# Six groups of an attention kernel hand a block of exponentials from VectorE to ScalarE, in a newly written order

## The chip, the cores and the metric

The kernel runs on one core of a Trainium2 chip. Its engines are TensorE (PE, matmul), VectorE (DVE), ScalarE (ACT), GpSimd (POOL) and SyncE (SP), which here issues the DMAs. The metric is the device time of one execution in microseconds (us), the median of three runs.

## The reference

A layer norm of x (2048 tokens, 640 features) feeds two branches: attention with 32 heads of 20 features, and a gated mixer with an MLP. The output is x plus their product.

```python
xn = _layernorm(x, axis=-1)
s = _A_ref(xn, A_wqkv, A_wo)                 # 32 heads, Dh 20: softmax(q k / sqrt(20)) v, then @ wo
g = _silu(_B_ref(xn, B_w1, B_w2, B_w3, B_w4))
return x + s * g

# _B_ref(x, w1, w2, w3, w4)
h = _gelu(_layernorm(x, axis=-1) @ w1)
...
hs = jnp.concatenate([g0, g1, g2, g3], axis=-1) @ w2   # quarters of h, shifted by 1, -1, 2, -2 tokens
x1 = x + hs
h2 = _gelu(_layernorm(x1, axis=-1) @ w3) @ w4          # w3: 640 x 1536, w4: 1536 x 640
return x1 + h2
```

## The kernel before, in words

**Groups.** The 32 heads go in eight quads of four. For each quad the 2048 queries go in four chunks of 512. One (quad, query chunk) is a group; there are 32. In a group, the scores of 16 key tiles of 128 keys are formed for four heads, exponentiated and multiplied with the values into one PSUM bank, number 7, which is not shared. The other seven PSUM banks hold scores and all other products in turn. `attn_quad` (L1366) writes a group out.

**Two ways to exponentiate.** A plain key tile (`score_act`) has two exponentials on ScalarE, each over two heads by 512 queries (`exp_act`, the activation at L1684, 128x1024), and one value product of four matmuls (L1424, or L1606 for blocks). A *block* is a pair of key tiles (`BLK`) in which each tile has two heads on ScalarE and two on VectorE (`score_both`, L1690). VectorE turns scores into the bits of an approximate exponential (L1707, 128x1024, from PSUM). `block_bits` (L1571) then makes three copies of these bits with other offsets (v = 1, 2, 3) and multiplies all four versions with the values, v = 0 and 1 with weight one, the others with scaled values (`VP`): four value products for VectorE's half (L1606), one for ScalarE's half (L1424). A copy runs on GpSimd (L1592) for the versions that `PP` names, else on VectorE (L1594).

**How many blocks.** `ND[quad][qc]` is the number of blocks of a group, and `UNITS` says how they are joined: blocks one and two share one buffer (copies of 4096), so do three and four; a fifth stands alone (copies of 2048). `PP` names copies of the first and the third block only, so the fifth block's three copies are all VectorE's. `order` (L592) lays the blocks and the remaining plain tiles of a group in sequence: with five blocks six plain tiles are left, with four there are eight. Entries of `NR` from 100 up name the plain tile (by its place among them, 100 + place) whose four heads share one activation of 128x2048 (L1661) instead of two of 128x1024.

**Repeats.** `AGAIN` maps (quad, query chunk, key tile, head) to how many more times the score matmul of that head is written over the same bank (`score_pair`, L1617, `times`).

**The second branch.** `run_b` adds its stages while the attention runs: w1 beside quad 0, w2 beside quad 1, w3 and w4 from quads 2 and 4 on. Their matmuls all go through `mm_tile` (L725). For w3, a slab of 640x128 is loaded for each of 12 column tiles and four token chunks, 48 loads of 160 KB through a ring of three buffers on SP's queue (L2078, in `b_w3`). Between these loads SP also issues the copies of queries (`qm`, four issues a group, L1382), the transposes and stores of finished heads (L1750 and L1763, four stores a group) and the loads of keys and queries of the next quad.

**Order.** The whole program is a list of tasks with reads and writes. Its order on every engine, and the PSUM bank and buffer of every task, are written out in the string `TABLE` (L2133), which `follow` (L219) reads: two characters for a task, one for each resource that it takes. While reading, `follow` gives each task a planned start and end, from the costs in the task calls (`c_act`, `c_dve`, `c_pe`, numbers), from `SYNC_LAT` (planned time from an engine's end to a waiting engine), from the spacing of row-tiled matmuls (`row_at + 4.0`), and for a DMA from its bytes, a fixed latency and `dlat`. `plan_sync` (L323) draws the semaphore waits from the order and drops those that another wait implies; it sorts by planned ends. `emit` writes the instructions. So a cost constant reaches the chip only by the order that was written with it, and by which of several waits is left out.

Of the kernel before, what the change touches and what calls it, by code (L numbers as in the profile page):

```python
# [14 lines left out]
SYNC_LAT = {"pe": 225.0, "act": 158.0, "dve": 136.0, "pool": 160.0, "sp": 60.0}  # L15
# [42 lines left out]
class Planner:  # L58
# [160 lines left out]
    def follow(self, table):  # L219
# [18 lines left out]
        at = 0  # L238
# [7 lines left out]
        while at < len(table):  # L246
# [11 lines left out]
            if e == "pe" and pe_mode and t.mode:  # L258
                st = max(row_at + 4.0, *(row_end[x] for x in range(4) if t.part >> x & 1))
# [218 lines left out]
class Cfg:  # L478
# [5 lines left out]
    def __init__(self, S=2048, D=640, H=32, F=1536):  # L484
# [100 lines left out]
        self.AGAIN = {(2, 2, 6, 1): 1, (6, 0, 8, 2): 1, (6, 0, 8, 3): 1, (7, 0, 0, 0): 1, (7, 0, 0, 1): 1, (7, 0, 1, 3): 1, (7, 0, 9, 0): 2, (7, 0, 9, 1): 2, (7, 1, 1, 0): 2, (7, 1, 2, 1): 1, (7, 1, 3, 0): 3, (7, 1, 3, 1): 1, (7, 1, 5, 1): 1, (7, 1, 8, 2): 2, (7, 1, 9, 0): 1, (7, 1, 12, 2): 1, (7, 1, 12, 3): 1, (7, 1, 14, 1): 1}  # L585
# [3 lines left out]
        self.PP |= {(0, 0, 1, 3), (0, 0, 1, 2)}  # L589

# [43 lines left out]
def c_act(n):  # L634
    return 68 + 0.8333 * n
# [13 lines left out]
class Gen:  # L649
# [995 lines left out]
    def score_rows(self, b, qc, kt, wide):  # L1645
# [14 lines left out]
        T("act", c_act(2048),  # L1660
# [18 lines left out]
    def exp_act(self, hs, sa, tag):  # L1679
# [3 lines left out]
        self.T("act", c_act(1024),  # L1683
# [369 lines left out]
    def b_w3(self, c0):  # L2053
# [8 lines left out]
        for ch in (c0, c0 + 1):  # L2062
# [12 lines left out]
            for fc in range(FC):  # L2075
# [3 lines left out]
                  writes=[A("W3s", ws)], is_dma=True, nbytes=KC * 128 * 128 * 2, name=f"ld_w3_{ch}_{fc}", stream=f"w3{ws}")  # L2079
# [54 lines left out]
    r"#9#6#:#;#,#%###&#<&R#=#>#?#@#A#B#C#D#l#'#($4#-#$#E#F#Z#[#]#)#G#H#I#J#.$`#2#^#*#w#+$?&S$S#f$J#e#g#h#p%n#m$K#i$M#q#n#j#r#K#L#M#N$L$N#o#k$O#s#x#O$v#%$&#P$T#Q#R$"  # L2134
    r"P#{#|#y#_$U#b$V#`#t#a#d$Q#}#z#v#u$R#~$#$W$(#S$q$%%$6$r$s${)$t$u%&#T$|$}$w%'$l%$x$y#U$~$m%($)$X$Y$$$*$Z$n$o%#$p#V#W#X&Q$+$[#Y#c#/$]$,$'$z&[#&]&^&_&`%`'%a%b%c%"
    r"g$%d$%%h$A$-$5$&$a$.$/%p%i$_$8&a$^%)(%.%%8)%j%*%9%:%/%0%+%,%=&%e#5$7$b$9&T'%k%-$0$2$3$@%;%1%2%>%?&U%3#%@%A%4%l$:%<$B&V%f&W&X&c(&d%5%6%7$c&j%%q%m&e&f&g&k&l&m%"
    r"r&$1&n&w)&x&y%t#%u$D$C&Y$;$E%s$<&o$F$>%v%w&z&{*@$*;(*?#&h%C$G$d*<)*A%%x&|'((')'*'+$f',&6)&7*8#*9$*=)&8&9*4(*:#*5)*6(%B&:%E$e$=$g$h'-$I%D&}(&~$H$i*+$**#'#'$'%"
    r"%F$*,$%G%P%%y$j$k&;%U)%V%W'&%Q*>&<%z%H%R%K(%L%M%N%I%O%Z&%S%X%[%]%Y%{'%^%|%T%}*2(%_%J*B&*C%*1'%~&#(H(I&&$&'&(&$&)&*';&#0(G'<'='>'?&+&-&.*3'*D)*.%&%*-&&H#%o*/#"
    r"'@&,(J&2%&I&J&K&L&3*]&*^%&M*J$*_&*K#*H(*I)*E&?#&@*M&A&N&B&C*L%&D&4)'/&*P$#4+#(&5*Q%+$)+%)*S*7*0*O&*N''0'1'2*F'3'4*V)*U(&q(&r&='*R'*W(*Y&*X'&>&s&t&u+.#*f)*g(+"
    r"/$&v*T*Z$+0#*a%&i*`&*i'I#'J'K'L'M*|#*b%'N'.*j)'d*}$'e*[*~'*k(*m&*l%'5#'6'7'8'9+1$*o+2#+&*n$*c'B(':+3(*d)+?&&/+@'*e('C'D*h'*G'E'F(K'U&+4*r'V'W&E'X'G+A)+8$+9%+"  # L2140
    r":&+*(++)+P+,%'Y'O#'P'Q'R'Z*p*{'S+6%'T+5&+S#+T$+('+'(+7#']$'^+V'_'`'a+F%+G&+Z$+Y#'H'b+)$+;+C'+D(&F$*q&Z*t+H(+i%+]'A*x+E&+R#&G+h&+Q$*z+U'&O$''+~(*u+k&P,#'+-*s,"
    r"&#,%$,$#+n%+o&+q(P+I'f$,'%+X(+W'+t'g+[$'c,~'h+=#(L,@&+<$+>&,A%'['i'j*w,B('k*y'l#*v+B+_(+`)+c#+a)+J+b$'m,2&,3%,5+^'n'o+d&+l)+m('p,(,0#&p+z,1$'q+p$,8&,9%+e+f',"
    r"4%+g('r$'s#7't,>$,;,=#,6&,7%+w+K&0'u'v+j)2d+}+L'w'x#'y,?',D(,:$,M#,N$,E)'z'{'|,l%,k&,F),<,P,H#,m#,G$,I$,T(,S),C+u'},d',e&,g%'~,V,f'+x+s+r,h$,i(-1(-0)+v+M-2%,"
# [129 lines left out]
```

## Time and profile before

| | |
|---|---|
| three runs | 791.79, 790.84, 791.46 us |
| median | 791.46 us |
| the profiled execution | 791.46 us, its span (first to last instruction) 789.7 us |
| granted TensorE clock, mean | 0.998 |
| exponentials of 128x1024 on ScalarE | 718, the first at 21.9 us, the last starting at 781.7 us |
| exponentials of 128x2048 | 13 |
| conversions on VectorE (L1707) | 276 |

Busy time is that of an engine's own instructions; matmuls are pipelined and their ends are modelled, so a busy TensorE is not TensorE at its peak. ScalarE's instructions overlap a little, so its busy time counts each moment once, while the mean duration of one is longer than its spacing. "Idle before" is the time in which an engine stood before instructions of a group, with the work that ended it. The chain of waits is followed back from the last instruction. In a table by stretches each row has the stretch, its length and the busy time and instruction count of each engine in it.

### The profile page before, as it was taken

What the parts mean: (1) busy time and instruction counts of PE and PEld (TensorE: products, weight loads), DVE (VectorE), ACT (ScalarE), POOL (GpSimd) and SP (SyncE); (2) the same over time, 40 slices, a digit from 0 to 9 for tenths busy, and PEclk for the clock granted to TensorE, in tenths of its full rate; (3) what the DMA queues carried; (4) which work ended last, traced back from release to release, by engine and by line L of the source; (5) the groups of instructions that cost most, each with busy time, mean ns of one, the idle gap of its engine ahead of it and who ended that gap; (6) DMA issues with size and microseconds to landing.
All of it is one profiled execution on the core that took longest, in us unless ns stands there. A gap on an engine that the chain in (4) does not pass through costs nothing.

```text
span 789.7 us, 27655 instructions
## 1 busy us (share of the span) xinstructions
PE 774.1 (98%) x12434; PEld 292.9 (37%) x12434; DVE 702.0 (89%) x936; ACT 761.0 (96%) x791; POOL 440.3 (56%) x238
## 2 busy tenths in 40 slices
PE   8999999999999999999999999999999999998997
PEld 4433333234444333333433433233334333332454
DVE  8889888989999999988988888898989899897986
ACT  7999999999999999999999999999999999999896
POOL 5666646552655647575473645647544545536742
PEclk9999999999999999999999999999999999999999
DMA  6213633244111324333332132343340213115343
GB/s 175 47 56 103 154 82 80 63 97 106 39 27 37 55 53 89 80 62 85 62 93 54 24 71 55 70 77 62 86 101 21 49 22 92 22 19 139 86 141 109
DMA packets 141349, 58.09 MB, mean 74 GB/s; under 512 B 113728, under 2 KB 136432, under 8 KB 141232
## 3 DMA queue, kind: packets, MB, share of 16 engines
q1 hardware_dynamic: 141232, 56.33, 31.4%
q8 instruction: 97, 1.59, 0.9%
q14 instruction: 20, 0.16, 0.1%
HBM read 34.70 MB, written 10.33 MB: 57 GB/s over the span
## 4 chain that ended last, share of the span: by engine, by line
PE 76%; ACT 19%; DVE 2%; DMA 1%; SPq 1%; issue 0%
PE psum L725 28%; PE psum L1615 22%; ACT arena L1684 18%; PE psum L1606 14%; PE psum L1424 9%; PE psum L1632 1%; DVE arena L1707 1%; DMA arena<-in_A_wqkv_dram 1%; ACT arena L1661 1%; PE psum L1481 1%; SPq L912 1%; DMA arena<-in_B_w_dram 1%; PE psum L1455 0%; DVE arena L1594 0%; DVE arena L1863 0%
## 5 line engine op out<-in xcount | busy, mean ns | idle before, releaser
L1684 ACT ACTIVATE arena<-psum 128x1024 bf16<-128x1024 f32 x718 | 671.9, 1035 | 16.3 <-PE psum L1615 13.1
L1592 POOL TENSOR_TENSOR arena<-arena 128x2048 int32<-128x2048 int32 x92 | 330.0, 3598 | 187.2 <-DVE arena L1594 123.1
L1707 DVE TENSOR_SCALAR arena<-psum 128x1024 uint16<-128x1024 f32 x276 | 335.8, 1221 | 52.3 <-PE psum L1615 48.4
L725 PE MATMUL psum<-arena 128*32 128x320 bf16 (+1 forms) x5808 | 335.0, 333 | 1.5 <-DMA arena<-in_B_w_dram 0.9
L1615 PE MATMUL psum<-arena 32*128 32x512 bf16 x1956 | 261.9, 384 | 4.9 <-DVE arena L1707 2.0
L1606 PE MATMUL psum<-arena 128*22 128x512 bf16 x2208 | 191.5, 381 | 0.0
L725 PEld LDWEIGHTS psum<-arena 128*32 128x32 bf16 x5808 | 135.2, 96 | 123.8 <-issue 55.7
L1615 PEld LDWEIGHTS psum<-arena 32*128 32x128 bf16 x1956 | 69.8, 91 | 229.6 <-ACT arena L1684 127.9
L1594 DVE TENSOR_SCALAR arena<-arena 128x4096 uint16<-128x4096 uint16 (+1 forms) x139 | 140.7, 1034 | 2.1 <-PE psum L1606 1.2
L1424 PE MATMUL psum<-arena 128*22 128x512 bf16 x1432 | 136.4, 382 | 0.4 <-ACT arena L1661 0.3
L1606 PEld LDWEIGHTS psum<-arena 128*22 128x22 bf16 x2208 | 50.2, 90 | 65.0 <-issue 42.0
L1741 POOL TENSOR_TENSOR arena<-arena 128x512 bf16<-128x512 f32 x30 | 41.0, 1366 | 59.8 <-DVE arena L1594 40.7
L1424 PEld LDWEIGHTS psum<-arena 128*22 128x22 bf16 x1432 | 34.4, 90 | 47.9 <-issue 28.6
L2083 DVE CAST arena<-psum 128x512 bf16<-128x512 f32 x48 | 32.7, 683 | 3.0 <-PE psum L725 2.1
L1291 DVE CAST arena<-psum 128x512 bf16<-128x512 f32 x40 | 27.0, 682 | 2.1 <-PE psum L725 1.7
L1906 POOL TENSOR_TENSOR arena<-arena 128x640 bf16<-128x640 bf16 x12 | 16.7, 1400 | 21.4 <-DVE arena L1531 7.9
L936 DVE BATCH_NORM_STATS2 arena<-arena 128x6 f32<-128x320 bf16 x54 | 24.8, 478 | 1.0 <-DMA arena<-in_A_x_dram 1.0
L1661 ACT ACTIVATE arena<-psum 128x2048 bf16<-128x2048 f32 x13 | 24.7, 1898 | 0.8 <-PE psum L1615 0.6
L1728 DVE STREAM_TRANSPOSE arena<-psum 128x512 f32<-128x512 f32 x30 | 21.3, 710 | 2.4 <-PE psum L1606 1.2
L1840 DVE SCALAR_TENSOR_TENSOR arena<-psum,arena 128x320 bf16<-128x320 f32 x32 | 15.3, 487 | 7.8 <-PE psum L725 7.5
L953 POOL TENSOR_SCALAR arena<-arena 128x640 bf16<-128x640 bf16 x16 | 14.0, 876 | 14.5 <-DVE arena L1594 13.2
L2090 ACT ACTIVATE arena<-arena 128x6144 bf16<-128x6144 bf16 x4 | 21.1, 5316 | 0.0
(135 smaller groups left out, 330.4 us busy)
## 6 DMA issues: line engine op xcount, KB each, us to landing
arena<-in_B_w_dram SPq DMA_DIRECT2D x48, 160.0 KB, 2.8
arena<-arena SPq DMA_DIRECT2D x124, 32.0 KB, 1.9
arena<-in_B_w_dram SPq DMA_DIRECT2D x4, 960.0 KB, 5.5
arena<-in_A_x_dram SPq DMA_DIRECT2D x8, 320.0 KB, 5.6
arena<-in_A_x_dram SPq DMA_DIRECT2D x16, 160.0 KB, 2.5
out_dram<-arena SPq DMA_DIRECT2D x16, 160.0 KB, 1.9
heads<-arena SPq DMA_DIRECT2D x120, 20.0 KB, 2.0
arena<-queries SPq DMA_DIRECT2D x28, 80.0 KB
```

The lines of the kernel that those rows point to most:

```text
L725: ins = e.matmul(pb[32 * c:32 * c + 32, 0:N], lhsT(k, c), rhs(k, c), start=(k == 0), stop=(stop and k == nk - 1), tile_position=(0, 32 * c))
L1291: T("dve", c_dve(512), lambda e, h=h, c=c: e.tensor_copy(KS[:, 512 * c:512 * c + 512], self.wbank(h)[:, 0:512]), reads=[wa], writes=[A("KS ...
L1424: ins = e.matmul(pb[32 * i:32 * i + 22, 0:512], VA[:, ql, kts[i // 2], i, :], PT[:, slots[i // 2][0].slot, slots[i // 2][0].at(i % 2):slot ...
L1592: return e.tensor_tensor(dst.bitcast(I32), U[:, ub, 0:w].bitcast(I32), bass.AP(c.tensor, c.offset, [list(c.ap[0]), [0, w // 2]]), op=ALU.add)
L1594: fa if onp else lambda e, v=v, dst=dst: e.tensor_scalar(dst, U[:, ub, 0:w], EXP_B[v], None, op0=ALU.add),
L1606: ins = e.matmul(pb[32 * i:32 * i + 22, 0:512], wv, dst[:, at:at + 512].bitcast(BF16), start=first, stop=final, tile_position=(0, 32 * i))
L1615: return e.matmul(out, self.KT[32 * i:32 * i + 32, b, 128 * kt:128 * kt + 128], q, start=True, stop=True, tile_position=(32 * i, 0))
L1661: lambda e: e.activation(self.PT[:, hp[0].slot:hp[0].slot + 2, :], self.psum[:, 512 * h0.slot:512 * h0.slot + 2048].rearrange("p (a b) -> ...
L1684: lambda e: e.activation(self.PT[:, hp.slot, :].rearrange("p (a b) -> p a b", b=512), self.banks(hs), AF.Exp, scale=cfg.scale),
L1707: return e.tensor_scalar(U[:, ub, 1024 * at:1024 * at + 1024].rearrange("p (a b) -> p a b", b=512), self.banks(hd), a_exp, EXP_BIAS, op0=A ...
L1741: return e.tensor_tensor(OnT.rearrange("p (k d a) -> p a k d", k=4, a=4), Ob[:, :].rearrange("p (a k d) -> p a k d", a=4, k=4), in1, op=AL ...
L2083: T("dve", c_dve(512), lambda e, h=h, fc=fc, i=i, G=G: e.tensor_copy(G[:, i, fc, :], self.wbank(h)[:, 0:512]), reads=[wa], writes=at, name ...
```

## The change

It does five things.

1. `ND` drops from five to four in the groups (1,2), (2,2), (3,2), (6,1), (6,3) and (7,1). `NR` is set to match in these groups: (6,1) and (7,1) name tile 107 instead of 105, which in both cases is the last plain tile; the other four have none.
2. `AGAIN` has nine entries with 14 repeats in place of 18 entries with 24.
3. Planned numbers: `SYNC_LAT` of TensorE 250 instead of 225, row spacing 8 instead of 4, each exponential 17 ns less.
4. Each slab of w3 is planned to land 1200 ns later (`dlat=1200.0`).
5. `TABLE` is another string throughout, 105 lines for 105: another order on the engines and other banks.

```diff
-SYNC_LAT = {"pe": 225.0, "act": 158.0, "dve": 136.0, "pool": 160.0, "sp": 60.0}
+SYNC_LAT = {"pe": 250.0, "act": 158.0, "dve": 136.0, "pool": 160.0, "sp": 60.0}
...
-                st = max(row_at + 4.0, *(row_end[x] for x in range(4) if t.part >> x & 1))
+                st = max(row_at + 8.0, *(row_end[x] for x in range(4) if t.part >> x & 1))
...
-        self.AGAIN = {(2, 2, 6, 1): 1, (6, 0, 8, 2): 1, (6, 0, 8, 3): 1, (7, 0, 0, 0): 1, (7, 0, 0, 1): 1, (7, 0, 1, 3): 1, (7, 0, 9, 0): 2, (7, 0, 9, 1): 2, (7, 1, 1, 0): 2, (7, 1, 2, 1): 1, (7, 1, 3, 0): 3, (7, 1, 3, 1): 1, (7, 1, 5, 1): 1, (7, 1, 8, 2): 2, (7, 1, 9, 0): 1, (7, 1, 12, 2): 1, (7, 1, 12, 3): 1, (7, 1, 14, 1): 1}
+        self.AGAIN = {(3, 3, 14, 2): 1, (7, 1, 5, 0): 1, (7, 1, 6, 0): 1, (7, 1, 7, 0): 3, (7, 1, 9, 0): 1, (7, 1, 9, 1): 1, (7, 1, 12, 0): 1, (7, 2, 6, 2): 1, (7, 2, 6, 3): 4}
         self.EARLY = 4
         self.ND = ([2, 4, 4, 4],) + tuple([5, 4, 5, 4] for _ in range(5)) + ([5, 5, 5, 5], [5, 5, 4, 4])
...
+        self.NR = [list(x) for x in self.NR]
+        self.NR[1][2] = ()
+        self.NR[2][2] = ()
+        self.NR[3][2] = ()
+        self.NR[6][1] = (107,)
+        self.NR[6][3] = ()
+        self.NR[7][1] = (107,)
+        self.ND = ([2, 4, 4, 4], [5, 4, 4, 4], [5, 4, 4, 4], [5, 4, 4, 4], [5, 4, 5, 4], [5, 4, 5, 4], [5, 4, 5, 4], [5, 4, 4, 4])
...
-        T("act", c_act(2048),
+        T("act", c_act(2048) - 17,
...
-        self.T("act", c_act(1024),
+        self.T("act", c_act(1024) - 17,
...
-                  writes=[A("W3s", ws)], is_dma=True, nbytes=KC * 128 * 128 * 2, name=f"ld_w3_{ch}_{fc}", stream=f"w3{ws}")
+                  writes=[A("W3s", ws)], is_dma=True, nbytes=KC * 128 * 128 * 2, dlat=1200.0, name=f"ld_w3_{ch}_{fc}", stream=f"w3{ws}")
...
```

What is left out is the string `TABLE`, old and new.

More of the change, by code (lines that the diff above doesn't have):

```diff
@@ L2137 @@
[L2137 to L2140, printed above, removed]
```

206 lines of the change are left out of this document (105 added, 101 removed).

## The prediction

> **What bounds the kernel now.** I read the page's busy times first, then the chain of waits, then the groups of instructions and the wait view, and last a table of stretches and the timeline of ScalarE.
>
> ```profile
> span 789.7 us, 27655 instructions
> ...
> PE 774.1 (98%) x12434; PEld 292.9 (37%) x12434; DVE 702.0 (89%) x936; ACT 761.0 (96%) x791; POOL 440.3 (56%) x238
> ...
> PE 76%; ACT 19%; DVE 2%; DMA 1%; SPq 1%; issue 0%
> ...
> L1684 ACT ACTIVATE arena<-psum 128x1024 bf16<-128x1024 f32 x718 | 671.9, 1035 | 16.3 <-PE psum L1615 13.1
> ```
>
> The wait view gives microseconds in all, times, longest:
>
> ```profile
> PEld psum L1615 <- ACT arena L1684: 127.9, 339, 0.8
> ```
>
> TensorE looks like the bound (98% busy, 76% of the chain), but its score matmuls at L1615 waited 339 times, 127.9 us in all, for an exponential of L1684 to empty a bank. ScalarE with 96% runs without a pause wherever it is fed. So the two are coupled through the seven PSUM banks, and ScalarE's idle time is what an order can still win. Its place is seen when the span is cut where ScalarE's work changes character: the start, quad 0, quads 1 to 3, quad 4, quad 5, quad 6, quad 7 but its last part, the end.
>
> ```profile
> core 0: us, PE busy (x) PEld busy (x) DVE busy (x) ACT busy (x) POOL busy (x), PEclk, DMA share, GB/s
> 0.00:35.55 35.55, 32.22 (x746) 17.01 (x750) 29.89 (x101) 29.41 (x49) 19.80 (x50) 1.00 0.51 118
> 35.55:117.68 82.13, 81.81 (x1155) 26.82 (x1147) 71.42 (x83) 82.04 (x88) 51.61 (x30) 1.00 0.39 96
> 117.68:404.70 287.02, 285.26 (x4366) 103.11 (x4370) 268.49 (x352) 281.38 (x281) 164.15 (x77) 1.00 0.31 67
> 404.70:493.40 88.70, 88.59 (x1453) 32.91 (x1444) 76.17 (x93) 88.63 (x94) 48.67 (x18) 1.00 0.27 57
> 493.40:581.80 88.40, 87.41 (x1246) 28.41 (x1242) 77.72 (x86) 86.68 (x94) 51.00 (x21) 1.00 0.38 72
> 581.80:677.70 95.90, 95.47 (x1513) 36.37 (x1501) 85.47 (x98) 93.77 (x90) 49.26 (x18) 1.00 0.23 54
> 677.70:760.00 82.30, 79.57 (x1362) 33.47 (x1362) 70.96 (x88) 76.88 (x79) 44.65 (x20) 1.00 0.30 76
> 760.00:789.70 29.70, 23.75 (x632) 14.77 (x624) 21.91 (x42) 22.20 (x24) 11.14 (x8) 0.96 0.42 131
> ```
>
> ScalarE's idle time is stretch minus ACT busy: 0.09 us in quad 0, 5.64 in quads 1 to 3, 0.07 in quad 4, 1.72 in quad 5, 2.13 in quad 6, 5.42 in quad 7 before its end. The start (6.14) and the end (7.50) hold none of the changed groups; I leave them. The sum in between is 15.1 us. VectorE's share is 87% and 86% where ScalarE has no gap (71.42 of 82.13, 76.17 of 88.70) and 94% in quads 1 to 3 (268.49 of 287.02).
>
> A little more idle time hides in instructions that overlap. Per exponential, from the same stretches with L1684 alone:
>
> ```profile
> core 0: us, ACT busy (x), PEclk, DMA share, GB/s
> ...
> 35.55:117.68 82.13, 78.63 (x85) 1.00 0.39 96
> 117.68:404.70 287.02, 252.43 (x271) 1.00 0.31 67
> 404.70:493.40 88.70, 83.20 (x90) 1.00 0.27 57
> ...
> 677.70:760.00 82.30, 67.17 (x72) 1.00 0.30 76
> ```
>
> That is 0.925 and 0.924 us each where it is fed, 0.931 and 0.933 in the two gappy stretches: 271 x 0.007 = 1.9 us and 72 x 0.008 = 0.6 us more to win there.
>
> **The change, part by part.** *Six fifth blocks.* The groups (quad, query chunk) (1,2), (2,2), (3,2), (6,1), (6,3), (7,1) have four blocks where they had five. A block is two key tiles; as a block, two exponentials on ScalarE, two conversions on VectorE (L1707), three copies (L1594; all on VectorE for a fifth block, 128x2048) and five value products of four matmuls; as plain tiles, four exponentials and two products. Prices come from the timeline of ScalarE, the groups by shape and the chain in order of time:
>
> ```profile
> 35.55 56.33 ACT L1684 ACTIVATE arena<-psum 128x1024 bf16<-128x1024 f32 x61
> ```
>
> ```profile
> L1707 DVE TENSOR_SCALAR arena<-psum 128x1024 uint16<-128x1024 f32 x276 | 335.8, 1221 | 52.3 <-PE psum L1615 48.4
> ...
> L1594 DVE TENSOR_SCALAR arena<-arena 128x2048 uint16<-128x2048 uint16 x48 | 31.9, 686 | 0.1
> ```
>
> ```profile
> 757.85 1.19 PE psum L1606 x20
> ```
>
> ScalarE: 61 exponentials in a row took 56.33 us; without the last one's own 1.035 that is 55.3 / 60 = 0.922 us each. Twelve more cost 12 x 0.922 = **+11.1 us**, all on the engine that has the least idle time; if none of it finds a gap the kernel is longer by that. VectorE loses 2 x 1.221 + 3 x 0.686 = 4.50 us a block, 27.0 us in all: 13.5 in quads 1 to 3 (then 255.0 us, 89% of the old stretch), 9.0 in quad 6 (76.5 of 95.9, 80%), 4.5 in quad 7. TensorE loses three products a block; 20 matmuls took 1.19 us in the chain, so 0.24 for four: 6 x 3 x 0.24 = 4.3 us. GpSimd's work is the same: the fifth block had no copy there. What VectorE and TensorE lose is no term of the sum by itself: it lies beside ScalarE's work, and counts only as idle time of ScalarE that it lets close.
>
> *Repeated score matmuls.* The dictionary of repeats holds 24 extra rounds before and 14 after, nearly all in quad 7: ten fewer, at up to 0.24 each, 2.4 us less for TensorE. If they all stood beside TensorE waits they are worth 0; I take none as a term of its own but let it count for quad 7 below.
>
> *Planner's numbers.* The TensorE wake-up (225 to 250), the row spacing (4 to 8), 17 off each exponential and 1200 more for a slab shape only planned times. On the chip they act through the written order and the waits drawn from it. The rows-wide entries change no count either: with five blocks only six plain tiles are left, so 111 and 113 of (2,2) and (3,2) were never reached, and 105 against 107 is the last tile in both.
>
> *Slabs of w3.* The chain in order of time, then the page's DMA and instruction groups, then the timeline show what a late slab costs now:
>
> ```profile
> 505.21 0.62 SPq L1763
> 505.82 0.04 issue
> 505.87 4.06 DMA arena<-in_B_w_dram
> ```
>
> ```profile
> L725 PE MATMUL psum<-arena 128*32 128x320 bf16 (+1 forms) x5808 | 335.0, 333 | 1.5 <-DMA arena<-in_B_w_dram 0.9
> ...
> arena<-in_B_w_dram SPq DMA_DIRECT2D x48, 160.0 KB, 2.8
> ```
>
> ```profile
> 510.06 0.61 PE L725 MATMUL psum<-arena 128*32 128x512 bf16 x8 [0.89 <-DMA arena<-in_B_w_dram]
> ...
> 511.13 1.02 ACT L1684 ACTIVATE arena<-psum 128x1024 bf16<-128x1024 f32 x1 [0.41 <-PE psum L1615]
> ```
>
> A slab issued behind a group's four stores (L1763, 0.62 us each) landed 4.06 us later instead of the median 2.8; TensorE stood 0.89 us and ScalarE 0.41 behind it. A plan that expects 1.2 us more puts such an issue earlier or its matmul later. The gain lies between 0 and quad 5's whole idle time, 1.7; I take 1.2, as the rest of that idle has no DMA in it. Moving a slab ahead of four stores delays these by one issue of at most 0.6 us; only a much later load of the stored heads reads them. A slab moved ahead of a group's four query loads delays that group's column-wise scores likewise, and ScalarE with them: a loss of up to 0.6 us each time. I take zero, since all of TensorE's waits at L725 for this tensor sum to 0.9, that one wait.
>
> *Order and banks.* Every instruction is placed anew, which no row of before prices. At best all 15.1 + 2.5 us of idle time between start and end go; at worst quads 0, 4 and 5, 259.2 us together, get gaps at the rate of quads 1 to 3 (5.64 / 287.02 = 2.0%), +5.1 us. I take the value between by stretch, nearest to what the gapless stretches do with VectorE at 86 to 87%: quads 1 to 3, of 7.5 us (5.64 + 1.9) 6.0 go, because VectorE falls from 94 to 89%; quad 6 has the split 5, 4, 5, 4 of the gapless quad 4, so 2.0 of 2.13 go; quad 7, of 6.0 (5.42 + 0.6) 4.0 go, TensorE having 0.7 + 2.4 us less to do there; quad 5, 1.2 of 1.72.
>
> Sum: +11.1 - 6.0 - 2.0 - 4.0 - 1.2 = **-2.1 us**. The profiled execution took 791.46 us, of which 789.7 is span and 1.8 lies around it; it equals the median of the three, 791.46. So 789.3 us.
>
> **The rivals.** *Slower: the gaps lie elsewhere.* The mechanism is ScalarE's queue alone: twelve exponentials lengthen six stretches that had little idle time of their own.
>
> ```profile
> 162.60:195.80 33.20, 33.08 (x544) 12.90 (x540) 30.38 (x37) 33.00 (x28) 14.27 (x5) 1.00 0.47 107
> 259.70:283.70 24.00, 23.65 (x346) 8.11 (x334) 23.70 (x35) 22.79 (x26) 16.54 (x6) 1.00 0.32 58
> 348.10:369.30 21.20, 21.20 (x303) 6.73 (x299) 17.75 (x24) 21.20 (x25) 15.44 (x6) 1.00 0.36 78
> 615.80:639.40 23.60, 23.56 (x377) 8.70 (x377) 20.37 (x24) 23.09 (x26) 12.11 (x4) 1.00 0.16 39
> 647.70:681.60 33.90, 33.76 (x502) 11.90 (x494) 30.17 (x35) 32.49 (x36) 17.39 (x7) 1.00 0.23 57
> 698.80:727.00 28.20, 25.72 (x356) 9.02 (x345) 21.74 (x23) 27.83 (x28) 14.19 (x6) 1.00 0.34 85
> sum 164.10, PE 160.97 PEld 57.36 DVE 144.12 ACT 160.39 POOL 89.93; mean PE 26.83 PEld 9.56 DVE 24.02 ACT 26.73 POOL 14.99
> ```
>
> From the first to the last exponential of each changed group ScalarE was idle 164.10 - 160.39 = 3.7 us. If only these gaps close, the sum is 11.1 - 3.7 = +7.4; with 1.2 for the slab and half a microsecond from quad 7's repeats it is +5.7: 797 us. For it: three of the six stretches have 0.0 to 0.4 us idle. Against it: projection work of the second branch is free to move between groups, so relief on VectorE in one stretch is used in the next. It decides once less than 11.1 us of idle time closes. Chance 0.30.
>
> *No difference.* The closing gaps just pay for the exponentials, within 0.2% (1.6 us, about what a measurement of this kernel can tell from no change): 791.5. It is the forecast with quads 1 to 3 giving 4.0 instead of 6.0. Chance 0.14 beside the share of the forecast that falls there.
>
> *All gaps close.* Quads 1 to 7 get the 0.1 us a quad of quads 0 and 4: 11.1 - 15.0 - 2.5 = -6.4, 785.1 us. For it are the gapless stretches; against it, quad 7's gaps follow from ever less filling work, not from VectorE. Chance 0.08.
>
> *The most loaded engine gets more.* No gap closes, each one being a hand-over between score matmuls and exponentials that the new order keeps: +11.1, 802.6 us. Waits on L1615 before the exponentials (13.1 us) speak for it, the gapless stretches against it. Chance 0.08. The Trainium skill, Perfetto Trace Analysis, "Identifying the Most-Contended Engine", speaks against this change in that way: it takes the engine of highest occupancy as the one to relieve, and for TensorE does not count matmul busy time; the trace agrees as to ScalarE's 96%, with TensorE's 98% set aside.
>
> *The slab edit does nothing.* The issue stays behind stores on SP's queue: 1.2 us of the sum gone, -0.9, inside the forecast's range.
>
> **How the numbers follow.** Forecast 0.40, its own range 786.5 to 791.0. Four fifths of it lie under 789.9 (0.2% below before): 0.32, with the case of all gaps 0.40 for faster. Same: 0.08 + 0.14 = 0.22. Slower: 0.30 + 0.08 = 0.38. For 8 in 10 the range reaches from 785.5, near the case of all gaps, to 798.0, over the main slower case; outside lie the last rival and some of each side's tail.
>
> **What would show it.** In the profile after: L1684 x730 at an unchanged 0.92 us, L1707 x264, the 128x2048 copies x30, L1606 x2112 and L1424 x1456, ACT busy near 772 us, VectorE near 675. Right: ScalarE's idle time in quads 1 to 3 under 2 us, in quad 6 under 0.5, in quad 7 near 2, and no wait of TensorE for a slab. Wrong: idle time that stays above 11 us between start and end, gaps in quads 0 and 4, or a start or end that moves by more than 1 us.

## The result and the profile after

Six runs of the changed kernel took 788.57 to 788.99 us, median 788.76; six of the kernel before, beside it, have a median of 791.62 us (790.66 to 792.77). The ratio of their means is 0.9964, with a 95% interval of 0.9951 to 0.9977: faster by 0.36%. The forecast was 789.3. The profiled execution has a span of 787.0 us against 789.7, so the profiles show 2.7 of the 2.9 us.

The functions at the end of the file stand 8 lines lower in the changed kernel: the exponential L1684 is now L1692, the conversion L1707 is L1715, the copy L1594 is L1602, the row scores L1615 are L1623, the block's product L1606 is L1614, the plain product L1424 is L1432, the column scores L1632 are L1640 and `mm_tile` L725 is L733. Its page, with the span, the busy times, the chain of waits and five groups of instructions:

```profile
span 787.0 us, 27583 instructions
...
PE 772.6 (98%) x12412; PEld 289.8 (37%) x12412; DVE 682.0 (87%) x906; ACT 765.8 (97%) x803; POOL 440.1 (56%) x238
...
PE 51%; ACT 47%; DVE 1%; issue 0%
...
L1692 ACT ACTIVATE arena<-psum 128x1024 bf16<-128x1024 f32 x730 | 678.6, 1092 | 10.0 <-PE psum L1623 6.1
...
L1715 DVE TENSOR_SCALAR arena<-psum 128x1024 uint16<-128x1024 f32 x264 | 321.4, 1220 | 61.0 <-PE psum L1623 57.0
L733 PE MATMUL psum<-arena 128*32 128x320 bf16 (+1 forms) x5808 | 330.6, 333 | 0.1
...
L1614 PE MATMUL psum<-arena 128*22 128x512 bf16 x2112 | 182.0, 381 | 0.0
...
L1432 PE MATMUL psum<-arena 128*22 128x512 bf16 x1456 | 139.2, 382 | 0.6 <-ACT arena L1692 0.5
```

These counts are those forecast. Another was not forecast: `TABLE` also chooses whether the score of a head is one matmul by rows or four by columns. 16 more scores go by columns, before and after:

```profile
L1632 PE MATMUL psum<-arena 128*32 128x512 bf16 x208 | 20.2, 380 | 0.0
```

```profile
L1640 PE MATMUL psum<-arena 128*32 128x512 bf16 x272 | 26.8, 382 | 0.1
```

ScalarE's share of the chain goes from 19% to 47%, TensorE's from 76% to 51%. ScalarE stood 10.0 us before exponentials instead of 16.3, and no product of L733 waits for a slab any more. TensorE's wait for the exponentials has not shrunk but grown, from 127.9 us in 339 times:

```profile
PEld psum L1623 <- ACT arena L1692: 151.7, 394, 0.8
```

So the sum of these waits does not measure lost time here: the kernel is faster with more of it. The stretches, cut at the same places of the work as before (start, quad 0, quads 1 to 3, quads 4, 5, 6, quad 7 but its end, the end):

```profile
core 0: us, PE busy (x) PEld busy (x) DVE busy (x) ACT busy (x) POOL busy (x), PEclk, DMA share, GB/s
0.00:35.01 35.01, 33.05 (x744) 16.95 (x744) 29.92 (x100) 29.59 (x49) 20.49 (x47) 1.00 0.59 144
35.01:116.75 81.74, 81.74 (x1149) 26.17 (x1148) 71.10 (x85) 81.55 (x87) 49.72 (x32) 1.00 0.35 89
116.75:407.00 290.25, 287.51 (x4384) 102.59 (x4376) 259.22 (x337) 285.49 (x288) 163.71 (x76) 1.00 0.30 65
407.00:495.60 88.60, 88.05 (x1449) 33.33 (x1441) 76.01 (x92) 88.08 (x95) 51.50 (x23) 1.00 0.29 60
495.60:582.70 87.10, 87.03 (x1249) 28.51 (x1245) 77.70 (x84) 86.05 (x93) 49.77 (x19) 1.00 0.36 73
582.70:678.80 96.10, 95.03 (x1524) 36.07 (x1520) 82.01 (x92) 95.99 (x94) 50.30 (x18) 1.00 0.22 52
678.80:757.30 78.50, 76.68 (x1322) 31.46 (x1318) 63.87 (x78) 76.82 (x81) 43.47 (x19) 1.00 0.30 77
757.30:787.00 29.70, 23.54 (x632) 14.73 (x628) 22.19 (x43) 22.26 (x24) 11.10 (x8) 0.98 0.43 136
```

How many exponentials lie in the stretches stands in the same stretches with L1692 alone (the count takes in the line's ACT_TABLE_LOAD instructions, two in quads 1 to 3 and one in quad 6, before as after):

```profile
core 0: us, ACT busy (x), PEclk, DMA share, GB/s
...
116.75:407.00 290.25, 256.94 (x277) 1.00 0.30 65
...
582.70:678.80 96.10, 81.01 (x89) 1.00 0.22 52
678.80:757.30 78.50, 67.86 (x74) 1.00 0.30 77
```

Of the same rows of before the prediction shows all but that of quad 6, which had four exponentials fewer:

```profile
581.80:677.70 95.90, 78.58 (x85) 1.00 0.23 54
```

Length after minus length before gives the second column of this table. The third is what the added exponentials cost (0.922 us each), the fourth their difference: what was closed.

| stretch | longer by | added exponentials | closed | forecast |
|---|---|---|---|---|
| start and quad 0 | -0.9 | 0 | 0.9 | 0 |
| quads 1 to 3 | **+3.2** | 6, 5.5 | **2.3** | **6.0** |
| quads 4 and 5 | -1.4 | 0 | 1.4 | 1.2 |
| quad 6 | +0.2 | 4, 3.7 | 3.5 | 2.0 |
| quad 7 to its end | -3.8 | 2, 1.8 | 5.6 | 4.0 |
| end | 0.0 | 0 | 0.0 | 0 |
| sum | -2.7 | 12, 11.1 | 13.8 | 13.2 |

The sum is near the forecast, its parts are not: 3.7 us too little in quads 1 to 3 and 4.2 too much elsewhere cancel, and that is luck. Quads 1 to 3, where most was to come from, got longer. Quad 6 and quad 7 gave more. ScalarE's idle time there (length minus ACT busy) is 0.11 and 1.68 us, but 4.76 in quads 1 to 3, where 5.64 had been. The timeline of ScalarE shows the change in the late quads in one row (start, length), from quad 6 into quad 7:

```profile
636.23 56.44 ACT L1692 ACTIVATE arena<-psum 128x1024 bf16<-128x1024 f32 x61
```

### The profile page after: what moved, and what is told of

Its sections match the earlier page's. It is cut to its first block, busy times and chain, and to the rows that moved or that the text cites. A ratio compares the mean times of both kernels' runs of the same rounds, so it can differ in the third digit from the quotient of the medians.

```text
span 787.0 us, 27583 instructions
## 1 busy us (share of the span) xinstructions
PE 772.6 (98%) x12412; PEld 289.8 (37%) x12412; DVE 682.0 (87%) x906; ACT 765.8 (97%) x803; POOL 440.1 (56%) x238
## 4 chain that ended last, share of the span: by engine, by line
PE 51%; ACT 47%; DVE 1%; issue 0%
ACT arena L1692 40%; PE psum L733 19%; PE psum L1623 15%; PE psum L1614 8%; PE psum L1432 6%; ACT arena L2098 3%; PE psum L907 1%; ACT arena L1669 1%; ACT arena L2006 1%; PE psum L1640 1%; ACT arena L2126 1%; PE psum L1489 1%; ACT L1692 0%; DVE arena L1715 0%; PE psum L1463 0%; PE psum L1079 0%
## 5 line engine op out<-in xcount | busy, mean ns | idle before, releaser
L1692 ACT ACTIVATE arena<-psum 128x1024 bf16<-128x1024 f32 x730 | 678.6, 1092 | 10.0 <-PE psum L1623 6.1
L1715 DVE TENSOR_SCALAR arena<-psum 128x1024 uint16<-128x1024 f32 x264 | 321.4, 1220 | 61.0 <-PE psum L1623 57.0
L733 PE MATMUL psum<-arena 128*32 128x320 bf16 (+1 forms) x5808 | 330.6, 333 | 0.1
L1623 PE MATMUL psum<-arena 32*128 32x512 bf16 x1930 | 257.1, 384 | 5.5 <-ACT arena L1692 3.0
L1614 PE MATMUL psum<-arena 128*22 128x512 bf16 x2112 | 182.0, 381 | 0.0
L733 PEld LDWEIGHTS psum<-arena 128*32 128x32 bf16 x5808 | 134.2, 96 | 122.5 <-issue 52.7
L1623 PEld LDWEIGHTS psum<-arena 32*128 32x128 bf16 x1930 | 69.7, 91 | 232.2 <-ACT arena L1692 151.7
L1432 PE MATMUL psum<-arena 128*22 128x512 bf16 x1456 | 139.2, 382 | 0.6 <-ACT arena L1692 0.5
L1602 DVE TENSOR_SCALAR arena<-arena 128x4096 uint16<-128x4096 uint16 (+1 forms) x121 | 130.1, 1089 | 4.2 <-PE psum L1614 3.4
L1614 PEld LDWEIGHTS psum<-arena 128*22 128x22 bf16 x2112 | 46.9, 90 | 57.6 <-issue 38.6
L1432 PEld LDWEIGHTS psum<-arena 128*22 128x22 bf16 x1456 | 35.1, 90 | 47.7 <-issue 32.0
L1640 PE MATMUL psum<-arena 128*32 128x512 bf16 x272 | 26.8, 382 | 0.1
```

Of the source, the lines that this page charges most:

```text
L733: ins = e.matmul(pb[32 * c:32 * c + 32, 0:N], lhsT(k, c), rhs(k, c), start=(k == 0), stop=(stop and k == nk - 1), tile_position=(0, 32 * c))
L1432: ins = e.matmul(pb[32 * i:32 * i + 22, 0:512], VA[:, ql, kts[i // 2], i, :], PT[:, slots[i // 2][0].slot, slots[i // 2][0].at(i % 2):slot ...
L1602: fa if onp else lambda e, v=v, dst=dst: e.tensor_scalar(dst, U[:, ub, 0:w], EXP_B[v], None, op0=ALU.add),
L1614: ins = e.matmul(pb[32 * i:32 * i + 22, 0:512], wv, dst[:, at:at + 512].bitcast(BF16), start=first, stop=final, tile_position=(0, 32 * i))
L1623: return e.matmul(out, self.KT[32 * i:32 * i + 32, b, 128 * kt:128 * kt + 128], q, start=True, stop=True, tile_position=(32 * i, 0))
L1640: ins = e.matmul(out[32 * c:32 * c + 32, :], self.KT[:, b, 128 * kt + 32 * c:128 * kt + 32 * c + 32], self.QM[:, gb, i, :], start=True, st ...
```

## The experiments

**Theory A** is the prediction's: ScalarE's queue sets the time, and a lighter VectorE lets its gaps close. Its **rival** says that no single engine sets it: relief of one finds the others right behind. **Theory C** came after b_thin and a_thin: TensorE's own work sets the time. The kernel before was run beside each of them; the runs on after are compared with after through it. `SIX` in the diffs is the set of the six changed groups, and "order unchanged" means that TABLE is the same string, so every instruction has its old place on its engine and its old bank.

| run | edit | median us | ratio to before, 95% | span |
|---|---|---|---|---|
| before | | 791.1 to 791.6 | | 789.7 |
| after | | 788.76 | 0.9964 (0.9951 to 0.9977) | 787.0 |
| b_exps | before, ScalarE loaded | 799.92 | 1.0116 (1.0092 to 1.0140) | 802.8 |
| b_dve | before, VectorE relieved | 791.01 | 0.9993 (0.9983 to 1.0003) | 789.1 |
| b_swap | before, both | 798.52 | 1.0107 (1.0081 to 1.0133) | 801.9 |
| b_slab | before, one slab moved | 791.58 | 0.9999 (0.9990 to 1.0007) | 789.2 |
| b_thin | before, ScalarE relieved | 790.47 | 0.9992 (0.9978 to 1.0006) | 788.7 |
| b_pe | before, TensorE relieved | 791.22 | 1.0004 (0.9995 to 1.0012) | 790.5 |
| b_all | before, all three relieved | 790.95 | 1.0007 (0.9991 to 1.0023) | 789.1 |
| b_order | before, another order | 792.02 | 1.0004 (0.9989 to 1.0018) | 788.8 |
| a_thin | after, ScalarE relieved | 787.13 | 0.9951 (0.9938 to 0.9964) | 785.1 |
| a_dve | after, VectorE loaded | 809.81 | 1.0237 (1.0214 to 1.0261) | 808.1 |
| a_pv | after, TensorE loaded | 790.93 | 0.9997 (0.9989 to 1.0006) | 789.9 |
| a_noagain | after, no repeats | 789.47 | 0.9974 (0.9965 to 0.9984) | 786.9 |

The ratio compares means, so it need not follow the medians; the span is that of one profiled execution. The granted TensorE clock was not the same in all executions. In the profile of b_exps it falls to 0.57 for 20 us (the last three numbers are the clock, the DMA share and GB/s):

```profile
720.00:740.00 20.00, 18.77 (x143) 3.90 (x141) 9.77 (x9) 15.62 (x20) 8.37 (x4) 0.57 0.43 122
```

That execution took 804.55 us at a mean clock of 0.987, three others of b_exps at 0.998 took 798.5 to 799.0. The profile of b_swap has the same fall at the same place. So the spans of these two runs are not to be compared with the others.

**The block edit in the old order.** b_exps lengthens ScalarE's work in the six groups, b_dve takes the fifth block's work from VectorE, b_swap does both; the order is unchanged.

b_exps cuts the two own exponentials of a fifth block into 12 pieces each, which costs ScalarE time without another instruction of any other engine:

```diff
 SIX = {(1, 2), (2, 2), (3, 2), (6, 1), (6, 3), (7, 1)}
...
-               lambda e: e.activation(self.PT[:, hp.slot, :].rearrange("p (a b) -> p a b", b=512), self.banks(hs), AF.Exp, scale=cfg.scale),
+               lambda e, cuts=(0, 86, 172, 258, 344, 430, 512) if tag in {f"{q}_{c}_{k}_{k}" for q, c in SIX for k in (0, 1)} else None: (
+                   e.activation(self.PT[:, hp.slot, :].rearrange("p (a b) -> p a b", b=512), self.banks(hs), AF.Exp, scale=cfg.scale) if cuts is None else
+                   [e.activation(self.PT[:, hp.slot, 512 * a + x:512 * a + y], self.banks(hs)[:, a, x:y], AF.Exp, scale=cfg.scale)
+                    for a in range(2) for x, y in zip(cuts, cuts[1:])][-1]),
```

> The kernel before, with 12 exponentials (two in each of the six changed groups, those of the fifth block) cut into twelve pieces each: the same result, only more ScalarE time, estimated at 0.9 to 1.1 us for each, 11 to 13 us in all. Theory A (ScalarE already paces most of the old order, and what a group adds there is not absorbed): +7 to +12 us. Rival B (the old order is paced by TensorE and VectorE, ScalarE's gaps absorb it): +0 to +4 us.

b_dve leaves the fifth block's conversions and copies 64 columns wide:

```diff
-                  fa if onp else lambda e, v=v, dst=dst: e.tensor_scalar(dst, U[:, ub, 0:w], EXP_B[v], None, op0=ALU.add),
+                  fa if onp else lambda e, v=v, dst=dst, n=64 if (quad, qc) in SIX and blocks[0][0] == 4 else w: e.tensor_scalar(dst[:, 0:n], U[:, ub, 0:n], EXP_B[v], None, op0=ALU.add),
...
-            return e.tensor_scalar(U[:, ub, 1024 * at:1024 * at + 1024].rearrange("p (a b) -> p a b", b=512), self.banks(hd), a_exp, EXP_BIAS,
+            n = 32 if (quad, qc) in SIX and kt < 2 else 512
+            return e.tensor_scalar(U[:, ub, 1024 * at:1024 * at + 1024].rearrange("p (a b) -> p a b", b=512)[:, :, 0:n], self.banks(hd, n), a_exp, EXP_BIAS,
```

> The kernel before, where VectorE's share of the fifth block is cut to a stub in the six groups (conversions 64 of 1024 columns, copies 64 of 2048), so VectorE has about 24 us less to do; ScalarE and TensorE do the same as before. These heads' weights are then stale data. Theory A (VectorE's relief closes gaps of ScalarE even in the old order): -1.5 to -4 us. Rival B (gaps come from the order alone): -0.5 to +0.5 us.

b_swap is both edits together:

> Both edits at once in the old order: VectorE about 24 us less, ScalarE about 11 to 13 us more, which stands for the block edit without the new order (TensorE keeps its work). Theory A (the exponentials cost in full, the new order is what closes the gaps): +4 to +9 us against before. Rival B (the block edit alone brings the gain): -1 to -4 us.

Loading ScalarE cost 8.4 us of median, and 7.1 in the executions at a clock of 0.998; its busy time rose by 8.8 (761.0 to 769.8). Relieving VectorE of 18.6 us of busy time (702.0 to 683.4) gave 0.5, and its interval reaches over no change. Both together cost 7.0 (6.6 in the executions at 0.998 or more). So most of the load counts, as theory A has it, but the relief that was to pay for it is worth next to nothing in this order. 7.0 is close to what the rival "the gaps lie elsewhere" priced (+5.7 to +7.4), though the load here was 8.8 us and not 11.1: that rival describes the block edit without a new order, as far as this stand-in goes.

**The slab.** b_slab moves only the issue of the slab that the prediction saw arrive late, on SP's queue:

```diff
 SP, in order
-stores of group (4,2) x4, ld_w3_2_6
+ld_w3_2_6, stores of group (4,2) x4
```

> The kernel before with one thing moved in its order: the slab of w3 that was issued behind a group's four stores goes ahead of them. Theory A: no TensorE wait for a slab in the profile, and -0.5 to -1.5 us. Rival: the wait only moves, within 0.3 us of before.

No change. The wait itself is a matter of the execution: in b_dve, where the slabs and SP's queue are those of before, the same matmuls wait for no slab.

```profile
L728 PE MATMUL psum<-arena 128*32 128x320 bf16 (+1 forms) x5808 | 335.0, 333 | 1.4 <-DMA arena<-in_A_wqkv_dram 1.4
```

The 0.9 us that the profile of before shows for it belongs to that execution: those of b_thin and b_pe, with the same order, do not have it there either.

**Relief and load in the new order.** a_thin leaves the 12 added exponentials 64 of 1024 columns wide, so it asks what ScalarE's work still costs once the change is made. b_thin does it with the fifth blocks' own 12 exponentials in the kernel before.

```diff
-               lambda e: e.activation(self.PT[:, hp.slot, :].rearrange("p (a b) -> p a b", b=512), self.banks(hs), AF.Exp, scale=cfg.scale),
+               lambda e, n=32 if tag in {f"{q}_{c}_{k}_{1 - k}" for q, c in SIX for k in (0, 1)} else 512: e.activation(self.PT[:, hp.slot, :].rearrange("p (a b) -> p a b", b=512)[:, :, 0:n], self.banks(hs, n), AF.Exp, scale=cfg.scale),
```

> The changed kernel, where the 12 exponentials that the change gave to ScalarE compute 64 of their 1024 columns (the rest of these weights is stale data), so ScalarE has about 9.6 us less to do in the six groups. Theory A (ScalarE paces the new order nearly everywhere): -7 to -10 us against the changed kernel. Rival B (TensorE or VectorE stands right behind it): -1 to -4 us.

> The kernel before, where 12 exponentials of the six groups (the fifth block's own) compute 64 of their 1024 columns: about 9.6 us less for ScalarE, as in the run beside it. Theory A (the old order was held in these groups by VectorE and TensorE too): -2 to -6 us against before, clearly less than the same cut brings in the changed kernel. Rival B (ScalarE paced the old order just as much): -7 to -10 us.

ScalarE's busy time fell by 8.2 us in a_thin (765.8 to 757.6) and by 8.4 in b_thin (761.0 to 752.6). Taking this from the engine that is busy 97% of the time gave 1.6 us of median (1.9 of span) after the change. Before it, it gave 1.1 us, less than either theory had, and the interval of the ratio reaches over no change. This is where theory A falls: with the order as it is, ScalarE's queue alone does not set the time. In the Trainium skill, Perfetto Trace Analysis, "Identifying the Most-Contended Engine", the engine of highest occupancy is the one to relieve. With matmul busy time set aside, that is ScalarE here, and these two runs do not agree that its relief shortens the kernel by much while the order stays: 1 to 2 us of 8.

a_dve loads VectorE again, by reductions over data that it uses anyway, three in each of the groups; the exponentials stay with ScalarE. Its busy time rises by 25.2 us (682.0 to 707.2); the change had taken 20.0.

```diff
+        if (quad, qc) in SIX and block == 2 and v == 1:
+            k = self.spared
+            self.spared += 1
+            e.tensor_reduce(self.spare[:, k:k + 1], src.bitcast(BF16), axis=AX.X, op=ALU.max)
...
+            if (quad, qc) in SIX and kt in (2, 3):
+                k = self.spared
+                self.spared += 2
+                e.tensor_reduce(self.spare[:, k:k + 2], self.banks(hd), axis=AX.X, op=ALU.max)
```

> The changed kernel with VectorE's load put back without its use: in each of the six groups two reductions over 128x1024 from PSUM and one over 128x2048, about 4.6 us a group, 28 us in all, with the order as it is. Theory A (the room on VectorE is what lets ScalarE run without gaps): +4 to +10 us against the changed kernel. Rival B (the new order alone closed the gaps, VectorE has room to spare): +0 to +2 us.

It cost 21 us, more than any theory had. Each group is cut from its first exponential to that of the next group; the first three of the six and their sum stand here for after, then four and the sum for this run (columns as in the table of stretches):

```profile
161.43:194.95 33.52, 33.35 (x564) 13.13 (x556) 28.84 (x35) 33.06 (x29) 15.77 (x6) 1.00 0.28 67
260.59:281.77 21.18, 20.86 (x290) 6.61 (x282) 20.04 (x31) 21.18 (x25) 12.59 (x5) 1.00 0.35 64
348.69:372.47 23.78, 23.64 (x338) 7.58 (x334) 18.75 (x28) 23.78 (x27) 16.49 (x7) 1.00 0.29 64
...
sum 154.93, PE 152.50 PEld 51.94 DVE 129.02 ACT 154.47 POOL 86.93; mean PE 25.42 PEld 8.66 DVE 21.50 ACT 25.75 POOL 14.49
```

```profile
161.35:197.08 35.73, 33.61 (x552) 13.05 (x548) 31.86 (x37) 33.24 (x28) 15.76 (x6) 1.00 0.29 63
262.73:287.59 24.86, 22.62 (x290) 6.72 (x282) 22.22 (x33) 21.57 (x24) 12.58 (x5) 0.93 0.27 54
356.38:382.45 26.07, 23.98 (x342) 7.52 (x334) 22.30 (x30) 24.11 (x26) 16.64 (x7) 1.00 0.26 58
628.22:645.83 17.61, 17.61 (x259) 5.75 (x257) 13.43 (x16) 16.58 (x18) 10.51 (x3) 0.92 0.18 40
...
sum 169.25, PE 156.55 PEld 52.54 DVE 143.94 ACT 156.29 POOL 86.64; mean PE 26.09 PEld 8.76 DVE 23.99 ACT 26.05 POOL 14.44
```

The groups took 14.3 us more for 14.9 us more of VectorE's busy time; the rest of the 21 us lies right behind them, where the other reductions run. Two of the groups, (2,2) and (6,1), had a granted clock of 0.93 and 0.92; the four at 1.00 took 9.4 us more for 12.1. The one execution at a mean clock of 0.998 took 808.49 us, 19.7 above after. In after, VectorE is only 83% busy in these groups (129.02 of 154.93). So a share of 83% was no room: in the new order most of what is put on VectorE there, some three quarters or more, comes out as time. The reductions stand right ahead of conversions and a copy, and two of three read the PSUM banks that the conversion reads. What the same load costs at another place is not tested.

a_noagain drops all 14 repeated score matmuls (`AGAIN = {}`):

```diff
-        self.AGAIN = {(3, 3, 14, 2): 1, (7, 1, 5, 0): 1, (7, 1, 6, 0): 1, (7, 1, 7, 0): 3, (7, 1, 9, 0): 1, (7, 1, 9, 1): 1, (7, 1, 12, 0): 1, (7, 2, 6, 2): 1, (7, 2, 6, 3): 4}
+        self.AGAIN = {}
```

> The changed kernel without its 14 repeated score matmuls. Theory A (they stand in TensorE's waiting time): within 0.5 us of the changed kernel. Rival (they cost what they last): -2 to -3 us.

Its span is 786.9 against 787.0; its median lies 0.7 us above that of after, a little outside theory A's half microsecond, and the two intervals overlap. The repeats cost nothing, as the prediction took them.

**TensorE's work, and the order.** The change also takes 18 value products from TensorE. b_pe takes just these away in the old order, a_pv gives as many back in the new one.

```diff
+                    slim = (quad, qc, v) in SLIM and j == 4 and not (first or final)
-                    for i in range(4):
+                    for i in range(3, 4) if slim else range(4):
...
+                        m = 32 if slim else 512
-                        ins = e.matmul(pb[32 * i:32 * i + 22, 0:512], wv, dst[:, at:at + 512].bitcast(BF16),
+                        ins = e.matmul(pb[32 * i:32 * i + 22, 0:m], wv, dst[:, at:at + m].bitcast(BF16),
```

`SLIM` names three versions v of the fifth block in each of the six groups.

> The kernel before, its order unchanged, with three of the fifth block's five value products in each of the six groups cut to one matmul of 32 columns: 18 products, about 18 x 0.2 = 3.6 us of TensorE's work that the change also removes. The output lacks what these products add. Theory C (TensorE's own amount of work sets the time, the other two follow it): 788.0 +- 0.8, 3 to 4 us below before. Rival (each engine is held by the others in a fixed order, so that relief of one brings little, as with VectorE and with ScalarE): 790.0 to 791.5.

```diff
+                    twice = (quad, qc) in SIX and kts in ((0, 0), (1, 1), (4, 4)) and not (first or final)
-                    for i in range(4):
+                    for i in [0, 1, 2, 3] * (1 + twice):
                         ins = e.matmul(pb[32 * i:32 * i + 22, 0:512], VA[:, ql, kts[i // 2], i, :],
```

> The kernel after, its order unchanged, with the value product of three plain key tiles (0, 1 and 4) in each of the six groups done twice: 18 products of four matmuls, 3.9 us that the change took from TensorE are given back. The output counts these key tiles twice. Theory C: +3.5 to +4.5 us on after, back at 792. Rival (TensorE waits enough beside the other engines that products are hidden): +0 to +1.5 us.

b_order keeps the kernel's blocks and repeats and has the change's planner numbers but one: the row spacing stays 4. Its TABLE (left out here) was searched for anew with these, from the old one. It has as many turns of TensorE between score matmuls by rows and matmuls by columns as before (1142, counted in the written order; after has 1114).

```diff
-SYNC_LAT = {"pe": 225.0, "act": 158.0, "dve": 136.0, "pool": 160.0, "sp": 60.0}
+SYNC_LAT = {"pe": 250.0, "act": 158.0, "dve": 136.0, "pool": 160.0, "sp": 60.0}
...
-        T("act", c_act(2048),
+        T("act", c_act(2048) - 17,
...
-        self.T("act", c_act(1024),
+        self.T("act", c_act(1024) - 17,
...
-                  writes=[A("W3s", ws)], is_dma=True, nbytes=KC * 128 * 128 * 2, name=f"ld_w3_{ch}_{fc}", stream=f"w3{ws}")
+                  writes=[A("W3s", ws)], is_dma=True, nbytes=KC * 128 * 128 * 2, dlat=1200.0, name=f"ld_w3_{ch}_{fc}", stream=f"w3{ws}")
...
```

> The kernel before with all its blocks and repeats, and only the planner's numbers of the change and an order and banks found anew with them: nothing is moved from VectorE to ScalarE, and TensorE has as many value products and as many changes between rows and columns as before. If the order alone brings the gain, it takes 787 to 789, like after. If the gain comes from the work that the fifth blocks give back (theory C: 18 products and 28 changes of TensorE less), it stays at 790.5 to 792.

b_pe shows no change at all, so theory C fails for the old order. a_pv costs 2.2 us by the medians, 2.6 by the ratios (0.9997 less 0.9964, times 791) and 2.9 by the spans, of about 3.9 that were added: between theory C and its rival, so in the new order more than half of such products lie on the path. b_order is no faster; single runs of it spread from 789.2 to 795.6 us. It is one order, found from the old one; that no order of the old blocks is faster is not shown. Nor is there a run for the 28 turns fewer of after by themselves.

**All three engines at once.** b_all joins the edits of b_dve, b_thin and b_pe.

> The kernel before, its order unchanged, with everything of the six fifth blocks taken away that the change touches, on three engines at once: their own 12 exponentials reduced to 64 of 1024 columns (about 10 us of ScalarE), their conversions and copies to 64 columns (about 19 us of VectorE as profiled), 18 value products to one matmul of 32 columns (3.6 us of TensorE). The output lacks what these key tiles add. One at a time these gave 1.1, 0.6 and 0.0 us. If each engine was held back by the other two, the three together are worth more than their sum: 785 to 788, about 3.6 us or more below before. If the time that the groups take is fixed by the hand-overs of the written order, they add up at most: 789.5 to 790.5, and only an order made for the lighter work can use it.

Next to nothing: the median lies 0.2 us below before, and the ratio of means is 1.0007. Five of its twelve executions had a granted clock of 0.990 to 0.992 and took 793.2 to 794.8 us; the other seven, at 0.996 to 0.999, have a median of 790.5, 0.6 below before, about what b_dve alone gave. The profiled one is of these seven. The six groups in the kernel before, then in b_all, cut and with columns as above:

```profile
162.60:194.00 31.40, 31.28 (x514) 12.25 (x510) 28.58 (x35) 31.20 (x26) 14.27 (x5) 1.00 0.44 100
259.70:281.50 21.80, 21.45 (x312) 7.39 (x304) 21.50 (x31) 20.80 (x23) 15.27 (x6) 1.00 0.35 64
348.10:370.20 22.10, 22.10 (x315) 6.94 (x311) 18.48 (x26) 22.10 (x26) 16.34 (x7) 1.00 0.37 81
615.80:632.90 17.10, 17.06 (x275) 6.23 (x275) 13.93 (x16) 16.60 (x18) 11.08 (x4) 1.00 0.22 53
647.70:677.70 30.00, 29.86 (x444) 10.49 (x436) 26.27 (x31) 29.55 (x33) 16.16 (x7) 1.00 0.26 64
698.80:727.90 29.10, 26.62 (x372) 9.50 (x364) 22.64 (x24) 28.73 (x29) 14.45 (x7) 1.00 0.35 86
sum 151.50, PE 148.37 PEld 52.79 DVE 131.42 ACT 148.98 POOL 87.57; mean PE 24.73 PEld 8.80 DVE 21.90 ACT 24.83 POOL 14.59
```

```profile
164.05:195.24 31.19, 31.06 (x510) 12.26 (x510) 26.41 (x34) 30.49 (x25) 14.25 (x5) 1.00 0.45 99
260.64:282.50 21.86, 21.51 (x312) 7.21 (x304) 20.67 (x32) 19.27 (x24) 15.31 (x6) 1.00 0.35 64
348.96:371.04 22.08, 22.08 (x315) 6.94 (x311) 17.59 (x25) 20.78 (x26) 16.32 (x7) 1.00 0.40 63
615.89:632.90 17.01, 17.01 (x275) 6.23 (x275) 11.62 (x16) 15.26 (x19) 11.66 (x4) 1.00 0.22 53
647.65:677.50 29.85, 29.71 (x444) 10.34 (x436) 23.84 (x31) 28.04 (x33) 16.90 (x7) 1.00 0.27 65
698.41:727.22 28.81, 26.47 (x373) 9.12 (x362) 20.72 (x24) 27.30 (x30) 14.68 (x7) 1.00 0.37 94
sum 150.80, PE 147.85 PEld 52.12 DVE 120.84 ACT 141.13 POOL 89.13; mean PE 24.64 PEld 8.69 DVE 20.14 ACT 23.52 POOL 14.85
```

VectorE does 10.6 us less in them and ScalarE 7.9, and they are 0.7 us shorter, none by more than 0.3. What was taken away turned into idle time: ScalarE's rose from 2.5 us (151.50 - 148.98) to 9.7 (150.80 - 141.13). TensorE's waits for exponentials stay what they were, 127.9 us before:

```profile
PEld psum L1621 <- ACT arena L1690: 127.4, 336, 0.8
```

What sets the pace in the old order is therefore not how long the fifth block's work takes. Which hand-overs set it is not told apart by these runs.

## Why the prediction was right, and where it was not

The time, the sign and the counts were right; a part of the reasoning was not, and the time came out by errors that cancel. The forecast treated the time as ScalarE's work plus ScalarE's idle time, to be closed by a lighter VectorE. a_thin and b_all show that neither ScalarE's load nor VectorE's sets the time by itself while the order stays.

*The price of the exponentials* held: the 61 in a row took 56.44 us, less the last one's 1.09 and divided by 60 that is again 0.922. Where the order is not rewritten, b_exps and b_swap show that most of such work is paid for.

*Quads 1 to 3, -6.0* is the step that failed: "of 7.5 us (5.64 + 1.9) 6.0 go, because VectorE falls from 94 to 89%". VectorE did fall to 89% (259.22 of 290.25), and 2.3 us closed. All of it closed in the three changed groups: they take 75.3 us before (31.40, 21.80 and 22.10 in the rows above) and 78.5 after (33.52, 21.18 and 23.78), 3.2 more for 5.5 us of exponentials. But of the 5.64 us idle only 1.2 had lain in them. The other 4.4 lay in the groups between, which kept their blocks, and 4.3 of it is still there. The two longest stretches between them, before and then after:

```profile
194.00:259.70 65.70, 65.67 (x1171) 28.11 (x1167) 63.16 (x93) 63.98 (x70) 35.20 (x16) 1.00 0.18 40
281.50:348.10 66.60, 65.89 (x884) 20.48 (x876) 63.79 (x82) 65.19 (x70) 39.16 (x19) 1.00 0.38 77
```

```profile
194.95:260.59 65.64, 65.08 (x1149) 27.95 (x1153) 60.09 (x87) 63.98 (x69) 35.46 (x16) 1.00 0.20 40
281.77:348.69 66.92, 66.21 (x895) 20.11 (x887) 60.73 (x73) 65.70 (x71) 41.65 (x22) 1.00 0.39 82
```

VectorE's relief did reach them, from 96% to 92 and 91% (63.16 of 65.70 and 63.79 of 66.60 to 60.09 of 65.64 and 60.73 of 66.92). ScalarE's idle time stayed: 1.72 and 1.41 us before, 1.66 and 1.22 after. So for these quads the rival's "the gaps lie elsewhere" is what happened. b_all points the same way: in the old order less work on VectorE, and on ScalarE and TensorE too, shortens its groups by 0.7 us in all. The idle share of ScalarE does not follow from VectorE's share. The 1.9 us of hidden idle time was also too large: the 271 instructions of that row are 269 exponentials and two ACT_TABLE_LOAD of 1.28 us, and without these it is about 1.1.

*Quad 6, -2.0 and quad 7, -4.0* were too small: 3.5 and 5.6. The forecast took them as gaps of ScalarE alone. Quad 6 closed more than the 2.13 us of idle time that it had, so exponentials there also came closer together. Its timeline has such rows before, then after:

```profile
632.91 13.29 ACT L1684 ACTIVATE arena<-psum 128x1024 bf16<-128x1024 f32 x14 [0.51 <-PE psum L1615]
```

```profile
609.66 25.02 ACT L1692 ACTIVATE arena<-psum 128x1024 bf16<-128x1024 f32 x27
```

Without the last one's own duration that is 0.94 us each, then 0.92. In quad 7 it is 0.917 (67.86 / 74) where it was 0.933. This is also why ACT busy is 765.8 us and not near 772: the 730 exponentials take 678.6 us, only 6.7 more than the 718 did.

*The slab, -1.2*: quads 4 and 5 became 1.4 us shorter, but this term was sized on a wait of 0.9 us that belonged to one execution, the profiled one of before, and most of the 1.4 is that wait. b_slab shows that the median holds nothing of it. The match is a coincidence of the profiled execution.

*VectorE, -27.0* was a sum of rows, and the rows held: the conversions fell by 14.4 us (335.8 to 321.4, priced 12 x 1.221) and the copies of 128x2048 by 11.8 (31.9 to 20.1, priced 18 x 0.686):

```profile
L1602 DVE TENSOR_SCALAR arena<-arena 128x2048 uint16<-128x2048 uint16 x30 | 20.1, 684 | 0.0
```

The engine's busy time fell by 20.0 only, 702.0 to 682.0. VectorE's instructions overlap as ScalarE's do: their durations add up to 755.0 us before and 729.1 after, so a fall of 25.9 in durations was 20.0 in busy time. Nothing in the forecast hung on it.

*TensorE's 4.3 us and the repeats, no term of their own*: right for the repeats (a_noagain), and for the products in the old order (b_pe). In the new order, products are worth 2.2 to 2.9 us of about 3.9 (a_pv), more than the forecast's "lies beside ScalarE's work".

*The start and the end* moved by 0.5 and 0.0 us, inside the bound of 1 us. Of the signs that the forecast named, quad 4 has a small gap (0.52 us where 0.07 had been), and quads 1 to 3 have 4.76 us idle where it said under 2.

*The rivals.* "The gaps lie elsewhere" is what happens without the new order (b_swap, +7.0 against +5.7 to +7.4). "The most loaded engine gets more" (+11.1) came nowhere. What decided between forecast and rival was the order, which the prediction had treated as a thing that no row prices. In the old order a lighter load on one engine, or on all three, could not be turned into time; a new order around the old blocks brought nothing in the one form tried; the lighter blocks with an order written for them brought 2.9 us. That the two are needed together is shown as far as these kernels go: one new order of the old blocks was tried, and b_swap is a stand-in for the blocks in the old order. Which of the lighter loads the new order uses most is shown only from the other side: VectorE's and TensorE's work, put back, costs most of its own duration, while a lighter ScalarE gives a fifth of what is taken (1.6 of 8.2).

## What to carry to other kernels

In a program whose order and buffers are written out, the work that an edit removes can be worth next to nothing until the order is rewritten for it (b_all: three engines lighter, at most 0.1%), while most of the work that it adds is paid at once (b_swap: +1.07%). So price an edit and its new order together, and do not read spare room from an engine's share: at 83% busy, most of what was added came out as time. To find out what a relief is worth in the order that stands, shrink the instructions in place; it takes one run an engine. It does not tell what a new order can make of the relief: b_all gave next to nothing, and the change gave 2.9 us. And before idle time is counted as a gain, see in which groups it lies: most of that of quads 1 to 3 lay where the edit was not.

## What was not expected of the hardware

An exponential of 128x1024 has a mean duration of 1092 ns after and 1035 before, at the same mean spacing of 0.922 us over 61 in a row. So the duration of a ScalarE instruction that overlaps its neighbour is no price, and its growth no loss.

The same order does not start the same way each time: the group (1,2) begins at 162.60 us in the profile of before and at 164.05 in b_all, while the lengths of the six groups agree within 0.3 us. Differences of about a microsecond in one profiled span need the medians beside them.

The granted clock can fall in a kernel that holds it in most of its executions: to 0.57 for 20 us in one of b_exps, and to a mean of 0.990 to 0.992 in five of twelve of b_all, while none of the 17 of before beside b_all lay under 0.997. Why is not shown. A ratio of means takes such executions in, and a median can hide them.
